# Routed attention with a hard-swish feed-forward: where the range check reads, and what stands between two users of one PSUM bank

## Chip, cores, metric

One core of a Trainium2 chip. The metric is the device time of one execution in microseconds (us), median of several runs. The engines are TensorE (PE, with its weight loads as PEld), VectorE (DVE), ScalarE (ACT), GpSimd (POOL) and SyncE (SP), which issues the transfers.

## The reference

Attention in which a query sees only the keys that share its nearest centroid, then a feed-forward block with a hard-swish:

```python
batch, n_heads, seq, head_dim = (4, 8, 768, 64); n_clusters = 16
n_tokens, d_model, d_ff = (3072, 512, 2048)

q_assign = np.argmax(np.einsum('bhsd,hcd->bhsc', q_n, c_n), axis=-1)
k_assign = np.argmax(np.einsum('bhsd,hcd->bhsc', k_n, c_n), axis=-1)
mask = q_assign[:, :, :, None] == k_assign[:, :, None, :]
scores = scale * np.matmul(q, k.transpose(0, 1, 3, 2))
scores = np.where(mask, scores, -1000000000.0)
attn = np.exp(scores - np.max(scores, axis=-1, keepdims=True))
attn = attn / (np.sum(attn, axis=-1, keepdims=True) + 1e-09)
x = np.matmul(attn, v)                     # (b, h, s, d) -> (b*s, h*d)
h = x @ w_in
g = h * np.clip(h + 3.0, 0.0, 6.0) / 6.0
out = g @ w_out
```

Inputs are float32, the two weight matrices float64.

## The kernel before

`fast_path` does the work without the row maximum, and at the end writes a flag, `ok`. Only where a check of ranges fails does `general_path` run afterwards and do it again in a safe way; it does not run with these inputs.

The heads go in 16 pairs. A pair g has 12 chunks of keys (two halves of the queries, `hf`, by six key tiles, `j`), numbered n = 12 g + 6 hf + j, 192 in all. The main loop takes two chunks in a pass, called a step below; r is n mod 12. The order within each engine is the order in which the program is written (`tc.manual_schedule()`), each engine works through its own list in that order, and the tile framework adds the waits. A step does, in this order:

- `scores` (L349) of the chunks n and n+1: products of queries and keys into `ps`, plus the routing part from `xm`; ScalarE's exponential into `ex` (L356); GpSimd adds `ex` up into `acc` (L360, L363).
- `attn_v` (L367) of the two chunks before: `ex` times the values into `pv`, copied to `num` after six chunks (L379).
- the range check left over from the step before (the list `later`).
- at r = 2 and r = 8, `divide` (L385) for the half that ended: PE sums `acc` over the keys into `pd` (L394), VectorE takes the reciprocal `rcp` (L398) and multiplies `num` with it into `xT` (L399). ScalarE's `in_range` (L406) adds up a copy, called `same`, of `pd` at once, and of `rcp` in the next step. The sums must stay finite and under a bound, which is tested at the end.
- the routing of the next pair ("prep", `prep_items`, L467), in pieces: `turn` (two pieces in each of r = 0 and r = 2, of three transposes each, `pqk`, copied to `xf` by VectorE or ScalarE), `route` (r = 4: 24 narrow matmuls `pr`, then VectorE's argmax into `one_hot`), `route_turn` (two pieces in r = 8 and one in r = 10: four matmuls each, `po`, cast to `xm` by ScalarE, L328).
- feed-forward items of a batch whose attention is done, from a list called `fill` (`ffn_items`, L416): an "up" item is four matmuls into `ph` (L423), ScalarE's Relu `t` (L430) and VectorE's `gT` (L432); a "down" item is four matmuls into `py` (L445). `items_by` (L495) says how many a step gets: none before n = 52, mostly one from n = 52 to 78, four from n = 80 to 98, two or three after that. Prep pieces and items alternate, and the piece comes first (L549 to L553).
- from the start until n = 80 also the weights: loads of float64 chunks and their decoding, two ScalarE passes and five VectorE operations for a chunk (L201 to L230).

PSUM has eight banks. `pd`, `pqk`, `pr` and `po` are short-lived and come from `scratch` (L164): from n = 52 on they share one bank (`psum_t`), one after another; before that every third of them takes this bank and the others take the two banks of the feed-forward items (`psum_m`). A new user of a bank waits until the last reader of the one before is through.

Of the kernel before, what the change touches and what calls it, by code (L numbers as in the profile page):

```python
# [8 lines left out]
F32 = mybir.dt.float32  # L9
BF16 = mybir.dt.bfloat16  # L10
U32 = mybir.dt.uint32
I32 = mybir.dt.int32
ALU = mybir.AluOpType
ACT = mybir.ActivationFunctionType
AX = mybir.AxisListType
# [3 lines left out]
P = 128  # L19
NCH = S // P  # L20
NC2 = 2 * NCH
HALF = S // 2
NHC = NCH // 2
NG = B * H
# [6 lines left out]
NW = NKT * DFF // WC + NFT  # L31
# [3 lines left out]
W_HIGH = 2.0**15  # L35
# [8 lines left out]
BOUND = 2.0**60  # L44
# [72 lines left out]
def fast_path(ctx, tc, ok, q, k, v, centroids, moe_w_in, moe_w_out, out):  # L117


    nc = tc.nc  # L120
    PSUM = bass.MemoryType.PSUM

    def pool(name, bufs, **kw):
        return ctx.enter_context(tc.tile_pool(name=name, bufs=bufs, **kw))

    const = pool("const", 1)
# [4 lines left out]
    smallp = pool("smallp", 2)  # L131
    expp = pool("expp", 4)
    accp = pool("accp", 2)
    nump = pool("nump", 2)
# [16 lines left out]
    ones = const.tile([P, D], F32, name="ones")  # L151
    rank = const.tile([P, C], F32, name="rank")
    half_c = const.tile([P, 1], F32, name="half_c")
    cnT = const.tile([P, H * C], F32, name="cnT")
    one_hot = const.tile([P, NC2, P], BF16, name="one_hot")


    totals = const.tile([P, 2, NG], F32, name="totals")
    w_totals = const.tile([P, 2, NW], F32, name="w_totals")
# [4 lines left out]
    def scratch(shape, name):  # L164

        st["scratch"] += 1
        if st["early"] and st["scratch"] % 3:
            return psum_m.tile(shape, F32, name=name, tag="m")
        return psum_t.tile(shape, F32, name=name, tag="t")
# [3 lines left out]
    def load(g, *names):  # L173
        if g >= NPAIR:
            return
        b, h = divmod(2 * g, H)
        for name in names:
            if name == "v":
                dst = st["v", g] = vp.tile([P, NCH, 2, D], F32, name="vt")
            elif name == "q":  # L180
                st["qk", g] = qkp.tile([P, 2, NCH, 2, D], F32, name="qk")
            if name != "v":
                dst = st["qk", g][:, "qk".index(name)]
            src = {"q": q, "k": k, "v": v}[name]
            for t in range(2):
                nc.sync.dma_start(dst[:, :, t], src[b, h + t].rearrange("(p j) d -> p j d", p=P))
# [9 lines left out]
    def load_weights(i):  # L196
        if i < len(chunks):
            st["raw", i] = rawp.tile([P, WC, 2], U32, name="raw")
            nc.sync.dma_start(st["raw", i], chunks[i][1])
# [37 lines left out]
    def constants():  # L237
        make_identity(nc, ident)
        nc.vector.tensor_copy(out=ident_q, in_=ident)
        nc.vector.tensor_scalar_mul(out=ident_k, in0=ident, scalar1=-FAR)  # L240
        for t in range(2):
            nc.vector.tensor_reduce(
                out=parity[:, t : t + 1],
                in_=ident.rearrange("p (h t c) -> p t h c", t=2, c=C)[:, t], axis=AX.XY, op=ALU.max,
            )
        for c in range(C):
            nc.gpsimd.memset(rank[:, c : c + 1], float(C - c))
        nc.gpsimd.memset(half_c, 0.5)
        nc.gpsimd.memset(ones, 1.0)
        nc.gpsimd.memset(w_low, W_LOW)  # L250
        nc.gpsimd.memset(one_hot, 0.0)

    def centroid_norm():
        cn = unit_rows(nc, smallp, cen, D)

        nc.scalar.activation(out=w_totals[:, 0, 0:1], in_=w_low, func=ACT.Exp)

        wide = smallp.tile([P, 2, D], F32, name="cenwide")
        for t in range(2):
            nc.vector.tensor_scalar_mul(out=wide[:, t], in0=cn, scalar1=parity[:, t : t + 1])  # L260
        pc = scratch([P, P], "pc")
        nc.tensor.transpose(out=pc, in_=wide, identity=ident)
        nc.vector.tensor_copy(out=cnT, in_=pc)
# [67 lines left out]
    def where(n):  # L331
        g, r = divmod(n, 2 * NCH)
        return (g, *divmod(r, NCH))

    def scores_qk(n):
        g, hf, j = where(n)
        st["ps", n] = psum_s.tile([P, 2, 512], F32, name="ps")
        scores_part(n, st["xf", g], True)
# [46 lines left out]
    def divide(n):  # L385
        g, hf, _ = where(n)
        b, kt = divmod(g, NKT)
        if kt == 0 and hf == 0:
            st["xT", b] = xtp.tile([P, NKT, S], F32, name="xT")
        acc, num = st.pop(("acc", g, hf)), st.pop(("num", g, hf))  # L390
        pd = scratch([P, 512], "pd")
        pd = pd[:, 0:HALF]
        for t in range(2):
            nc.tensor.matmul(  # L394
                pd[t * D : (t + 1) * D], lhsT=ones, rhs=acc[:, t], start=True, stop=True
            )
        rcp = nump.tile([P, HALF], F32, name="rcp")
        nc.vector.reciprocal(out=rcp, in_=pd)  # L398
        nc.vector.tensor_tensor(  # L399
            out=st["xT", b][:, kt, hf * HALF : (hf + 1) * HALF], in0=num, in1=rcp, op=ALU.mult  # L400
        )
        in_range(g, hf, 0, pd)
        return lambda: in_range(g, hf, 1, rcp)


    def in_range(g, hf, a, x):  # L406
        same = nump.tile([P, HALF], BF16, name="same", tag="same")
        nc.scalar.activation(  # L408
            out=same, in_=x, func=ACT.Copy, accum_out=totals[:, a, 2 * g + hf : 2 * g + hf + 1]
        )  # L410


# [54 lines left out]
    def prep_items(g, r):  # L467

        if g >= NPAIR:
            return []  # L470
        if r in (0, 2):
            return [lambda: turn(g, r), lambda: turn(g, r + 1)]
        return {
            4: [lambda: route(g)],
            8: [lambda: route_turn(g, 0), lambda: route_turn(g, 1)],
            10: [lambda: route_turn(g, 2)],
        }.get(r, [])
# [27 lines left out]
    fill, later = [], []  # L505
    done = 0

    with tc.manual_schedule():
        nc.scalar.dma_start(cen, centroids.rearrange("h c d -> (h c) d"))
        load(0, "q", "k")  # L510
        constants()
        load(0, "v")
        load_weights(0)
        centroid_norm()
        for part in range(4):
            turn(0, part)
        load(1, "q", "k")
        scores_qk(0)
        scores_qk(1)
        route(0)  # L520
        for part in range(3):
            route_turn(0, part)

        for n in range(0, total + lag_d + 2, 2):
            g, r = divmod(n, per_pair)
            for i in (n, n + 1):
                if i < total:
                    scores(i)
            for i in (n - lag_v, n - lag_v + 1):
                if 0 <= i < total:  # L530
                    attn_v(i)
            for check in later:
                check()
            later = []
            m = n - lag_d + 1
            if m >= 0 and m % NCH == NCH - 1:
                later.append(divide(m))
            if n == READY:
                st["early"] = False
            if m >= 0 and m % per_batch == per_batch - 1:  # L540
                fill += ffn_items(m // per_batch)
            if r == 6:
                load(g + 2, "q", "k")
                load(g + 1, "v")
            prep = prep_items(g + 1, r)
            want = items_by(n + 2) - done if n < total else len(fill)
            want = min(want, len(fill))
            done += want
            for i in range(max(len(prep), want)):  # L549
                if i < len(prep):  # L550
                    prep[i]()
                if i < want:
                    fill.pop(0)()  # L553
            for i in range(chunks_by(n), chunks_by(n + 2)):
                load_weights(i + 1)
                decode_weights(i)
            if n >= total:
                for check in later:
                    check()
                later = []  # L560

    good = smallp.tile([P, 2 * NG], F32, name="good")
    fit = smallp.tile([P, 2 * NW], F32, name="fit")
    nc.vector.tensor_scalar(
        out=good, in0=totals.rearrange("p a n -> p (a n)"), scalar1=BOUND, scalar2=None, op0=ALU.is_le
    )
    for a, bound in enumerate((W_HIGH, 0.0)):
        nc.vector.tensor_scalar(  # L570
            out=fit[:, a * NW : (a + 1) * NW], in0=w_totals[:, a], scalar1=bound, scalar2=None,
            op0=ALU.is_le,
        )
    low = smallp.tile([P, 2], F32, name="low")
    nc.vector.tensor_reduce(out=low[:, 0:1], in_=good, axis=AX.X, op=ALU.min)
    nc.vector.tensor_reduce(out=low[:, 1:2], in_=fit, axis=AX.X, op=ALU.min)
    one = smallp.tile([P, 1], F32, name="one")
    nc.vector.tensor_reduce(out=one, in_=low, axis=AX.X, op=ALU.min)
    pl = psum_t.tile([1, P], F32, name="pl", tag="t")
# [365 lines left out]
```

## Time and profile before

| | |
|---|---|
| median of 3 runs | 1275.11 us (1271.45 to 1277.72) |
| the profiled execution, its own time | 1268.65 us |
| its span, first to last instruction | 1266.7 us |
| mean granted TensorE clock | 0.946 |
| PE busy | 1143.7 us |
| DVE, ACT, POOL busy | 392.8, 362.4, 299.0 us |

The profile is one execution. Its views: busy time by engine; waits, each put down to the instruction that ended it; groups of instructions by source line; the timeline of single instructions; and busy time with the granted TensorE clock for any stretch of time. A clock of 1.00 is 2.4 GHz, 0.50 is 1.2 GHz. Times in the timeline count from the first instruction. A matmul in float32 shows as two records, and the time of one record is longer than its distance to the next, since they are pipelined: the length of a group is read from the start of what follows it.

### The profile page before, as it was taken

Reading aid. Unit: us, or ns where it says so; the run is one execution under the profiler, and the core shown is the slowest. Engines: PE = TensorE matmul, PEld = TensorE weight load, DVE = VectorE, ACT = ScalarE, POOL = GpSimd, SP = SyncE. Lnnn points to the kernel's source line nnn. Section 1 sums busy time; section 2 is a strip of 40 time slices with the busy share of each in tenths; the row PEclk is TensorE's granted clock in tenths of the full one; section 3 lists DMA queues with packets and bytes.
Section 4 is the critical chain, followed back from the end, with each engine's and each line's share of the span. In section 5 each row is a group of like instructions: output and inputs, shape, how many; then the busy total and the mean of one; then the engine's idle time right before and its main releaser. Section 6 shows DMA issues by size and latency. Waiting matters only on the chain.

```text
span 1266.7 us, 11458 instructions
## 1 busy us (share of the span) xinstructions
PE 1143.7 (90%) x4610; PEld 575.1 (45%) x4610; DVE 392.8 (31%) x530; ACT 362.4 (29%) x692; POOL 299.0 (24%) x186
## 2 busy tenths in 40 slices
PE   6988878788989899888998889988899899999997
PEld 4444443334445435454444544545435444554553
DVE  3667886867012211222022211222111221210110
ACT  3555545444112211332223222232222331120110
POOL 3555632323111211221222212122121222000000
PEclk9998978889999999998999989999999999999999
DMA  5322242423001001010010100101000000000000
GB/s 129 82 72 61 71 121 67 121 67 71 8 25 30 1 17 46 1 38 1 17 46 1 38 1 18 46 1 38 1 17 21 1 1 8 17 1 17 9 9 20
DMA packets 83535, 42.81 MB, mean 34 GB/s; under 512 B 76304, under 2 KB 76304, under 8 KB 83472
## 3 DMA queue, kind: packets, MB, share of 16 engines
q1 hardware_dynamic: 83328, 41.95, 12.7%
q8 instruction: 38, 0.62, 0.2%
q14 instruction: 25, 0.20, 0.1%
q10 hardware_dynamic: 144, 0.03, 0.0%
HBM read 35.68 MB, written 6.29 MB: 33 GB/s over the span
## 4 chain that ended last, share of the span: by engine, by line
PE 81%; DVE 16%; ACT 2%; issue 1%; POOL 0%; DVEq 0%; POOLq 0%; ACTq 0%
PE py L445 27%; PE ph L423 27%; PE ps L344 11%; PE pv L373 9%; DVE rcp L398 6%; PE pr L290 3%; PE pqk L276 2%; DVE wunit L227 2%; DVE wunit L223 1%; PE pd L394 1%; DVE wtop L220 1%; DVE w_in_sb L230 1%; ACT same L408 1%; DVE wtop L216 1%; PE po L324 1%; DVE w_out_sb L230 1%
## 5 line engine op out<-in xcount | busy, mean ns | idle before, releaser
L363 POOL TENSOR_TENSOR acc<-acc,ex 128x768 f32<-128x768 f32 x128 | 237.7, 1857 | 557.4 <-ACT ex L356 552.3
L423 PE MATMUL ph<-xT,w_in_sb 128*128 128x384 f32 x1024 | 368.8, 518 | 0.0
L445 PE MATMUL py<-w_out_sb,gT 128*128 128x512 f32 x768 | 349.6, 611 | 0.0
L423 PEld LDWEIGHTS ph<-xT,w_in_sb 128*128 128x128 f32 x1024 | 202.7, 203 | 139.4 <-issue 28.5
L445 PEld LDWEIGHTS py<-w_out_sb,gT 128*128 128x128 f32 x768 | 148.6, 198 | 176.2 <-issue 175.7
L356 ACT ACTIVATE ex<-ps 128x768 f32<-128x768 f32 x192 | 151.5, 808 | 221.6 <-PE ps L344 221.1
L344 PE MATMUL ps<-xf 64*128 64x384 f32 x768 | 173.3, 531 | 7.2 <-ACT ex L356 7.2
L430 ACT ACTIVATE t<-ph,half_c 128x384 f32<-128x384 f32 x128 | 74.3, 580 | 354.5 <-PE ph L423 354.5
L432 DVE SCALAR_TENSOR_TENSOR gT<-t,ph 128x384 f32<-128x384 f32 x128 | 70.8, 554 | 305.7 <-ACT t L430 305.7
L373 PE MATMUL pv<-ex,vt 128*64 128x384 f32 x768 | 147.2, 505 | 0.0
L398 DVE RECIPROCAL rcp<-pd 128x384 f32<-128x384 f32 x32 | 81.8, 2555 | 119.3 <-PE pd L394 119.2
L360 POOL TENSOR_TENSOR acc<-ex 128x768 f32<-128x768 f32 x32 | 58.7, 1834 | 211.5 <-ACT ex L356 211.4
L451 DVE COPY y<-py 128x512 f32<-128x512 f32 x24 | 16.6, 692 | 273.9 <-PE py L445 273.9
L344 PEld LDWEIGHTS ps<-xf 64*128 64x128 f32 x768 | 66.1, 194 | 76.4 <-issue 52.6
L373 PEld LDWEIGHTS pv<-ex,vt 128*64 128x64 f32 x768 | 47.3, 138 | 83.8 <-issue 81.3
L276 PE MATMUL pqk<-ident,qk 128*128 128x128 f32 x192 | 35.7, 314 | 38.5 <-ACT same L408 32.7
L344 PE MATMUL ps<-xm 64*128 64x384 bf16 x384 | 65.6, 336 | 0.3 <-ACT xm L328 0.3
L408 ACT ACTIVATE same<-pd 128x384 bf16<-128x384 f32 x32 | 15.7, 490 | 152.6 <-DVE rcp L398 152.6
L324 PE MATMUL po<-ident_q,one_hot 128*128 128x128 bf16 x96 | 11.2, 243 | 53.1 <-ACT same L408 50.1
L276 PEld LDWEIGHTS pqk<-ident,qk 128*128 128x128 f32 x192 | 24.8, 157 | 66.7 <-ACT same L408 39.4
L290 PEld LDWEIGHTS pr<-cnT,xf 128*128 128x128 f32 x384 | 45.8, 198 | 12.2 <-ACT same L408 5.7
L324 PEld LDWEIGHTS <-one_hot 128*128 128x128 bf16 x192 | 13.9, 104 | 81.9 <-issue 77.9
(67 smaller groups left out, 496.1 us busy)
## 6 DMA issues: line engine op xcount, KB each, us to landing
raw<-in_moe_w_in_dram SPq DMA_DIRECT2D x16, 512.0 KB, 3.7
raw<-in_moe_w_out_dram SPq DMA_DIRECT2D x16, 512.0 KB, 3.5
qk<-in_q_dram SPq DMA_DIRECT2D x32, 192.0 KB, 3.5
qk<-in_k_dram SPq DMA_DIRECT2D x32, 192.0 KB, 4.2
vt<-in_v_dram SPq DMA_DIRECT2D x32, 192.0 KB, 4.4
out_dram<-y SPq DMA_DIRECT2D x24, 256.0 KB, 2.0
cen<-in_centroids_dram ACTq DMA_DIRECT2D x1, 32.0 KB, 1.7
```

The costliest lines, as they stand in the source:

```text
L276: nc.tensor.transpose(out=pt[:, i], in_=qk[:, j // NCH, j % NCH], identity=ident)
L290: nc.tensor.matmul(pr[:, j], lhsT=xf[:, j], rhs=cnT[:, c0 : c0 + 2 * C], start=True, stop=True)
L344: nc.tensor.matmul(st["ps", n][:, t, 0:HALF], lhsT=x[r, NCH + j], rhs=x[r, hf * NHC : (hf + 1) * NHC], start=first, stop=not first,)
L356: nc.scalar.activation(out=ex, in_=sc, func=ACT.Exp, scale=SM_SCALE)
L360: nc.gpsimd.tensor_tensor(out=acc, in0=st["ex", n - 1], in1=ex, op=ALU.add)
L363: nc.gpsimd.tensor_tensor(out=acc, in0=acc, in1=ex, op=ALU.add)
L373: nc.tensor.matmul(pv[t * D : (t + 1) * D], lhsT=vt[:, j, t], rhs=ex[:, t], start=(j == 0), stop=(j == NCH - 1),)
L398: nc.vector.reciprocal(out=rcp, in_=pd)
L423: nc.tensor.matmul(hh, lhsT=w_in_sb[:, kt, f * P : (f + 1) * P], rhs=xT[:, kt, hf * HALF : (hf + 1) * HALF], start=(kt == 0), stop=(kt == ...
L430: nc.scalar.activation(out=t, in_=hh, func=ACT.Relu, bias=half_c, scale=1.0 / 6.0)
L432: nc.vector.scalar_tensor_tensor(out=gT, in0=t, scalar=1.0, in1=hh, op0=ALU.min, op1=ALU.mult)
L445: nc.tensor.matmul(py, lhsT=st["g", f][:, i * P : (i + 1) * P], rhs=w_out_sb[:, f], start=(f == 0), stop=(f == NFT - 1),)
```

## The change

Three things. First, both passes of the range check read `rcp` in SBUF, and both are done in the step after the divide, behind that step's exponentials: a sum of `rcp`, which must stay under the bound, and a sum of Relu(1/BOUND - rcp), which must be 0. `pd` in PSUM is read by the reciprocal alone. Second, in a step the feed-forward item comes first and the prep piece second. Third, the two tests at the end are written as one loop, with a VectorE comparison more. The attention, routing and feed-forward arithmetic is the same.

```diff
@@ constants()
+        nc.gpsimd.memset(low_c, 1.0 / BOUND)
@@ divide(n)
-        in_range(g, hf, 0, pd)
-        return lambda: in_range(g, hf, 1, rcp)
-    def in_range(g, hf, a, x):
+        return lambda: in_range(2 * g + hf, rcp)
+    def in_range(i, rcp):
         same = nump.tile([P, HALF], BF16, name="same", tag="same")
+        nc.scalar.activation(out=same, in_=rcp, func=ACT.Copy, accum_out=totals[:, 0, i : i + 1])
+        lack = nump.tile([P, HALF], BF16, name="lack", tag="same")
         nc.scalar.activation(
-            out=same, in_=x, func=ACT.Copy, accum_out=totals[:, a, 2 * g + hf : 2 * g + hf + 1]
+            out=lack, in_=rcp, func=ACT.Relu, bias=low_c, scale=-1.0, accum_out=totals[:, 1, i : i + 1]
         )
@@ the main loop
             for i in range(max(len(prep), want)):
+                if i < want:
+                    fill.pop(0)()
                 if i < len(prep):
                     prep[i]()
-                if i < want:
-                    fill.pop(0)()
@@ the end
-    good = smallp.tile([P, 2 * NG], F32, name="good")
-    fit = smallp.tile([P, 2 * NW], F32, name="fit")
-    nc.vector.tensor_scalar(
-        out=good, in0=totals.rearrange("p a n -> p (a n)"), scalar1=BOUND, scalar2=None, op0=ALU.is_le
-    )
-    for a, bound in enumerate((W_HIGH, 0.0)):
-        nc.vector.tensor_scalar(
-            out=fit[:, a * NW : (a + 1) * NW], in0=w_totals[:, a], scalar1=bound, scalar2=None,
-            op0=ALU.is_le,
-        )
+    good = smallp.tile([P, 2, NG], F32, name="good")
+    fit = smallp.tile([P, 2, NW], F32, name="fit")
+    for got, sums, high in ((good, totals, BOUND), (fit, w_totals, W_HIGH)):
+        for a, bound in enumerate((high, 0.0)):
+            nc.vector.tensor_scalar(
+                out=got[:, a], in0=sums[:, a], scalar1=bound, scalar2=None, op0=ALU.is_le
+            )
...
```

How this moves instructions, at two places. (The added lines shift the line numbers: L394 is L396 in the changed kernel, L276 is L278, L423 is L426.)

PE at the divide in the step n = 110, one of the steps with three items. Before:

```order
L373 MATMUL pv<-ex,vt 64x384 x4
L394 MATMUL pd<-acc,ones 64x384 x2
L276 MATMUL pqk<-ident,qk 128x128 x3
L423 MATMUL ph<-xT,w_in_sb 128x384 x4
L276 MATMUL pqk<-ident,qk 128x128 x3
L423 MATMUL ph<-xT,w_in_sb 128x384 x8
```

and in the changed kernel:

```order
L375 MATMUL pv<-ex,vt 64x384 x4
L396 MATMUL pd<-acc,ones 64x384 x2
L426 MATMUL ph<-xT,w_in_sb 128x384 x4
L278 MATMUL pqk<-ident,qk 128x128 x3
L426 MATMUL ph<-xT,w_in_sb 128x384 x4
L278 MATMUL pqk<-ident,qk 128x128 x3
L426 MATMUL ph<-xT,w_in_sb 128x384 x4
```

An up item now stands between `pd` and the transposes that take its bank, and one stays between the two groups of transposes.

PE at the divide in the step n = 62, which has one item. Before:

```order
L394 MATMUL pd<-acc,ones 64x384 x2
L276 MATMUL pqk<-ident,qk 128x128 x3
L423 MATMUL ph<-xT,w_in_sb 128x384 x4
L276 MATMUL pqk<-ident,qk 128x128 x3
L344 MATMUL ps<-xf 128x384 x2
```

and in the changed kernel:

```order
L396 MATMUL pd<-acc,ones 64x384 x2
L426 MATMUL ph<-xT,w_in_sb 128x384 x4
L278 MATMUL pqk<-ident,qk 128x128 x6
L346 MATMUL ps<-xf 128x384 x2
```

The one item has gone ahead of both groups, so that nothing is left between them.

## Rows read from the trace of the kernel before

**Rows 1.** The page's head and busy time of PE (share of the span, instructions)

```profile
span 1266.7 us, 11458 instructions
...
PE 1143.7 (90%) x4610; PEld 575.1 (45%) x4610; DVE 392.8 (31%) x530; ACT 362.4 (29%) x692; POOL 299.0 (24%) x186
```

**Rows 2.** PE's waits: line, releaser, us in total, times, longest us

```profile
PE po L324 <- ACT same L408: 55.8, 13, 9.5
PE pqk L276 <- ACT same L408: 32.7, 10, 3.3
PE ps L344 <- ACT ex L356: 7.2, 4, 2.3
...
PE pqk L276 <- DVE xf L281: 5.7, 2, 2.9
...
PE ps L344 <- ACT xm L328: 0.3, 1, 0.3
```

**Rows 3.** Waits of all engines: ScalarE's check

```profile
ACT same L408 <- DVE rcp L398: 152.6, 32, 20.3
```

**Rows 4.** Timeline of one divide (start, us, engine, instruction, idle before and releaser)

```profile
590.85 0.81 PE L394 MATMUL pd<-acc,ones 128*64 128x384 f32 x4
...
591.71 2.56 DVE L398 RECIPROCAL rcp<-pd 128x384 f32<-128x384 f32 x1 [13.06 <-PE pd L394]
594.30 0.49 ACT L408 ACTIVATE same<-pd 128x384 bf16<-128x384 f32 x1 [3.82 <-DVE rcp L398]
...
594.94 0.59 PE L324 MATMUL po<-ident_q,one_hot 128*128 128x128 bf16 x4 [3.27 <-ACT same L408]
```

**Rows 5.** Timeline of PE: an up item, `pr`, two down items

```profile
541.57 2.75 PE L423 MATMUL ph<-xT,w_in_sb 128*128 128x384 f32 x8
544.15 0.49 PE L276 MATMUL pqk<-ident,qk 128*128 128x128 f32 x3
...
567.64 2.87 PE L290 MATMUL pr<-cnT,xf 128*128 128x32 f32 x24
...
580.63 7.13 PE L445 MATMUL py<-w_out_sb,gT 128*128 128x512 f32 x16
587.70 0.92 PE L344 MATMUL ps<-xf 64*128 64x384 f32 x4
```

**Rows 6.** By stretch: us, busy PE, PEld, DVE, ACT, POOL, then clock, DMA

```profile
168.00:307.00 139.00, 107.84 (x504) 55.35 (x500) 105.30 (x145) 68.17 (x152) 41.85 (x22) 0.88 0.36 96
375.00:1004.00 629.00, 579.93 (x2305) 291.68 (x2305) 125.07 (x175) 158.47 (x279) 137.46 (x76) 0.95 0.08 19
1004.00:1092.00 88.00, 88.00 (x306) 40.31 (x306) 12.71 (x16) 18.72 (x33) 19.92 (x12) 1.00 0.02 7
...
594.94:598.36 3.42, 3.42 (x8) 1.84 (x8) 0.00 (x0) 0.58 (x1) 0.00 (x0) 0.51 0.02 5
...
422.52:425.94 3.42, 3.42 (x17) 2.18 (x17) 0.00 (x0) 0.89 (x2) 0.00 (x0) 1.00 0.02 5
...
570.64:574.14 3.50, 3.50 (x7) 1.88 (x6) 2.76 (x6) 0.00 (x0) 0.00 (x0) 0.55 0.00 0
...
541.00:546.00 5.00, 5.00 (x21) 3.14 (x20) 1.11 (x2) 1.43 (x3) 1.61 (x1) 1.00 0.00 0
```

**Rows 7.** Timeline around n = 56, and PE's wait at n = 80

```profile
185.39 0.58 PE L324 MATMUL po<-ident_q,one_hot 128*128 128x128 bf16 x4 [9.41 <-ACT same L408]
...
186.01 0.58 ACT L328 CAST xm<-po 128x512 bf16<-128x512 f32 x1 [0.67 <-PE po L324]
...
312.51 0.59 PE L324 MATMUL po<-ident_q,one_hot 128*128 128x128 bf16 x4 [5.08 <-ACT same L408]
```

**Rows 8.** Timeline before n = 52: ScalarE at a divide, PE at another

```profile
43.26 0.49 ACT L408 ACTIVATE same<-pd 128x384 bf16<-128x384 f32 x1 [3.81 <-DVE rcp L398]
...
77.43 0.39 PE L324 MATMUL po<-ident_k,one_hot 128*128 128x128 bf16 x4 [2.87 <-ACT same L408]
```

**Rows 9.** Groups by line and shape: the check's pass over `rcp` (busy us, mean ns)

```profile
L408 ACT ACTIVATE same<-rcp 128x384 bf16<-128x384 f32 x32 | 16.6, 519 | 0.0
L408 ACT ACTIVATION_READ_ACCUMULATOR same<-rcp 128x1 f32 x32 | 6.3, 198 | 0.0
```

**Rows 10.** Timeline of the end: the first test of the sums, and `pl`

```profile
1217.77 0.20 DVE L566 TENSOR_SCALAR good<-totals 128x64 f32<-128x64 f32 x1
...
1257.65 0.27 PE L580 MATMUL pl<-ident,one 128*1 128x128 f32 x1
```

More of the change, by code (lines that the diff above doesn't have):

```diff
@@ L153, in fast_path @@
     half_c = const.tile([P, 1], F32, name="half_c")
+    low_c = const.tile([P, 1], F32, name="low_c")
     cnT = const.tile([P, H * C], F32, name="cnT")
@@ L560, in fast_path @@
                 later = []
-    good = smallp.tile([P, 2 * NG], F32, name="good")
-    fit = smallp.tile([P, 2 * NW], F32, name="fit")
-    nc.vector.tensor_scalar(
-        out=good, in0=totals.rearrange("p a n -> p (a n)"), scalar1=BOUND, scalar2=None, op0=ALU.is_le
-    )
-    for a, bound in enumerate((W_HIGH, 0.0)):
-        nc.vector.tensor_scalar(
-            out=fit[:, a * NW : (a + 1) * NW], in0=w_totals[:, a], scalar1=bound, scalar2=None,
-            op0=ALU.is_le,
-        )
+    good = smallp.tile([P, 2, NG], F32, name="good")
[5 more added lines that the diff above has]
+            )
     low = smallp.tile([P, 2], F32, name="low")
-    nc.vector.tensor_reduce(out=low[:, 0:1], in_=good, axis=AX.X, op=ALU.min)
-    nc.vector.tensor_reduce(out=low[:, 1:2], in_=fit, axis=AX.X, op=ALU.min)
+    nc.vector.tensor_reduce(out=low[:, 0:1], in_=good, axis=AX.XY, op=ALU.min)
+    nc.vector.tensor_reduce(out=low[:, 1:2], in_=fit, axis=AX.XY, op=ALU.min)
     one = smallp.tile([P, 1], F32, name="one")
```

## Prediction

> **What bounds the kernel now.** I read the page's first part, then TensorE's waits, one divide in the timeline, and the clock by stretches, in that order. TensorE (PE) is busy 90% of the span and the others under a third [rows 1], so time can be won where PE stands still or runs at its lower clock. PE's waits [rows 2] show who holds it: ScalarE's pass `same` (L408) ended 55.8 us of waits before `po` and 32.7 us before `pqk`, in 23 places, out of some 123 us in which PE is idle at all. `same` itself stood 152.6 us behind the reciprocal, in all 32 divides [rows 3]. One divide shows why [rows 4]: PE ends `pd` at 591.66, the reciprocal reads the bank from 591.71 to 594.27, ScalarE reads it after that, not beside it, and at 594.94 the bank is free for `po`: 3.27 us with PE idle. A timeline of PE alone lists the 23: 16 of exactly 3.27 and one of 5.08 from 307 us on, two of 3.27 and two of about 9.4 between 168 and 307 us, two of 2.9 to 2.8 earlier; a wait of 2.6 before `pr` is like them.
>
> The idle time costs twice. In the 3.42 us after that wait PE is granted 0.51 of its clock, close to its lower level of 1.2 GHz [rows 6]; the same view of the stretch after each of the 16 waits of 3.27 gives 0.50 to 0.63 for 15 of them, and 1.00 after 422.52. From 375 to 1004 us the mean is 0.95: 629 x 0.05 = 31 us lost, of which three stretches after `pr` such as 570.64 to 574.14 at 0.55 take 3 x 3.5 x 0.45 = 4.7. About 27 hang on the waits.
>
> **The change, part by part.** A step is one pass of the loop over n, r is n mod 12.
>
> *Stage C, from n=80 (307 to 1004 us).* All 17 divides with a routing piece behind them have three or four feed-forward items in their step. Now an item stands between `pd` and the piece, and another between the two pieces. An up item takes PE from 541.57 to 544.15, 2.58 us; two down items take 7.07, one 3.5 [rows 5]. The bank is free when the reciprocal ends, 2.6 us after `pd`, plus some 0.06: without ScalarE's pass 0.67 earlier than now [rows 4]. So an up item leaves 0.1 us of wait and a down item none. Saved: 16 x 3.27 + 5.08 = 57.4, less about 1 for the up items and 0.9 at n=80, whose reciprocal comes late (5.08 - 0.67 - 3.5 [rows 7]): 55.5 us. The items themselves are not added, only moved, and between two scratch users one item stays. Clock: 27 plus some 3 for n=80 and 86 (before 375 us), of which I take 28, since PE has no gap left there; from 1004 to 1092 us, with PE busy 88.00 of 88, it is 1.00 [rows 6]. C gives 83 us. What is late next is VectorE: the first item's `gT` queues behind reciprocal and `xT`, done some 3.9 us after `pd` (2.6 + 0.6 + 0.6 and gaps); the third item, which needs that item's bank, starts after 5.6 us, so this covers.
>
> *Stage B, n=52 to 78 (168 to 307 us).* Nearly every step has one item only, and two pieces in r = 0, 2, 8. Now the item is ahead of both and the second piece waits for the copy of the first: `po` to the end of its copy is 0.67 + 0.58 after PE's own 0.3 [rows 7], about 0.95 us of new wait. At n=56 and 68 PE waited 9.4, because VectorE was still decoding weights: the item (2.6) and `same` (0.67) come out, 0.95 comes in, -2.3 each. At n=62 and 74: 3.27 becomes 0.1 + 0.95, -2.2 each. At n=60 and 72 the wait for VectorE's copy `xf` was 2.9 each already [rows 2]; the item's `gT` (0.55) now queues ahead of that copy, +0.55 each. Sum -7.9. Clock: 0.88 over 139 us is 16.7 lost [rows 6]; at n=62 and 74 PE's gap falls under 1 us, which I take to return 1.7 each; the 6 us left at n=56 and 68 keep theirs low. B gives 11 us, bounds 0 (VectorE, 76% busy there, sets the pace and PE's gain turns into waits for it) and 17.
>
> *Stage A, before n=52 (40 to 168 us).* No items exist, so the order stays; only the check moves. ScalarE no longer stands behind the reciprocal ahead of its casts and exponentials (3.81 us at 43.26 [rows 8]). The four waits of scores for `ex`, 7.2 us in all [rows 2], came from that; I take all of them, and 0.67 from each of three waits for `same` (77.43 is one [rows 8]), and 2 for the clock. A gives 11 us; bounds 2 (only the 0.67s) and 14.
>
> *The new check.* Still two ScalarE passes in each of 32 divides, now both two steps' work later, behind that step's exponentials. The Relu pass is not in the trace with this shape; the nearest row, the Copy from the same tile, is 519 ns and its read-out 0.2 [rows 9], so about 0.7 us stands in front of that step's `t` or casts. With an item's 2.6 us on PE ahead of them this is hidden; in A, without items, it could cost up to 0.7 x 8 = 5.6, inside A's bounds. One more small VectorE comparison at the end sits at 1217.77, 40 us before the last chain `pl` at 1257.65 [rows 10]: nothing. A memset of one column more at the start: nothing, behind other memsets.
>
> Sum: 83 + 11 + 11 = 105 us. The profiled execution took 1268.65 us, 6.5 under the median 1275.11; the waits recur in every execution, so I take them off the median: **1170 us**.
>
> **The rivals.** *R1, the gap closes but the clock does not come back.* In 8 of C's 17 divides the piece behind the gap is six small transposes, in r = 2, and small pieces stay close together. After `pr`, of 24 narrow matmuls, the clock falls in three pairs though PE had no gap [rows 5, 6]. If the r = 2 divides stay low: 8 x 1.5 = 12 us, 1182; if all 17: 28 us, 1198. Against it: from 541 to 546 us, r = 0, both `pqk` pieces run between items at a clock of 1.00 [rows 6], the very order that r = 2 now gets. The Trainium skill's "TensorE: Matmul & The Clock Gate", Part 4 on PE-mode transposes, says that a transpose does not count as PE being busy in the same way, so that full clock does not engage for it: by that rule R1 is the outcome, with the 1182; the 1.00 of that row speaks against it as long as items surround the transposes.
>
> *R2, the single bank hands the wait on.* In steps with one item the two pieces now meet, and if VectorE's queue (decode, `gT`) stands in front of the copy as it did for 2.9 us at n=60, six steps of B pay up to 3 us instead of 0.95: 6 x 2 = 12, and B turns from -11 to about 0. With A at its lower end too the time is 1170 + 11 + 9 = 1190.
>
> *R3, the change does not do what it says:* the moved item cannot start in the gap, because its own bank or weights are late. Then only the 0.67 of 24 waits and A's exponentials go, 16 + 7: 1252. Against it: the item's two banks are a different pool, and no wait of PE for `t` or `gT` stands among its waits.
>
> *R4, slower: the prep becomes the chain.* Every routing piece now starts one item later. If what it feeds were needed at once, PE would stand for that item: 5 prep steps x 8 pairs in C x 3 us = 120, against 105 saved: 1290. It decides where the slack behind a piece is under one item, 2.6 us. The trace has `pr` at 567.64 and its first user `po` at 594.94 [rows 4, 5], 27 us later, and scores waited for `xm` 0.3 us once in all [rows 2].
>
> **How the numbers follow.** Forecast 0.78; R1 0.12; R2 0.05; R3 0.03; R4 0.02. Forecast's own bounds: C idle 52 to 57, C clock 22 to 33 (the three `pr` stretches may go or be joined by others), A 2 to 14, B 0 to 17; not all at one end, so 1153 to 1187. The range reaches on to R1's far end and R2, 1152 to 1198, and leaves out R3, R4 and the corner where all terms are low. A measurement here tells about 0.5% (6 us) from no change. Faster by more than that: the first four cases, 0.98, less 0.02 for R3 with A's part gone too: 0.96; same 0.02; slower, R4, 0.02.
>
> **What would show it.** Right: waits of PE for ScalarE's check gone from the list; in C nothing longer than 0.3 us between `pd` and the piece; clock near 0.99 from 307 us to the end of C, which should last about 614 us instead of 697; in B waits of `po` and `pqk` for `xm` and `xf` of about 1 us, six of them, and 6 us at n=56 and 68; in A no waits for `ex`. Wrong: low clock after r = 2 divides (R1), long waits for `xf` (R2), `pd` followed by idle time with the item behind it (R3), waits of scores for `xm` or of `po` for `one_hot` (R4).

## The result and the profile after

Predicted 1170 us, in 1152 to 1198; measured 1165.38 us median (1162.96 to 1167.33) against 1274.67 for the kernel before: a ratio of 0.914, 95% interval 0.911 to 0.917. The profiled execution took 1166.84 us, its span is 1164.7, its mean clock 0.977 (0.946 before).

The waits of PE in the changed kernel, in the columns of [rows 2]:

```profile
PE po L326 <- DVE rcp L400: 15.1, 2, 9.1
PE pqk L278 <- DVE xf L283: 8.8, 4, 3.1
...
PE ps L346 <- ACT ex L358: 4.8, 2, 3.2
PE po L326 <- DVE one_hot L314: 4.6, 3, 3.0
PE pqk L278 <- DVE rcp L400: 3.3, 1, 3.3
PE po L326 <- ACT xm L330: 1.3, 2, 0.7
PE pr L292 <- DVE rcp L400: 0.9, 1, 0.9
PE ps L346 <- ACT xm L330: 0.3, 1, 0.3
```

ScalarE's check, 55.8 and 32.7 us in [rows 2], is gone. What is left lies before n=80. The largest, 15.1 us in two places, is the reciprocal that VectorE reaches late at n=56 and 68.

The stages are cut at the start of four reciprocals, those of n=8, 50, 80 and 182, which both kernels have. Busy time and clock by stretch, in the columns of [rows 6], A, B, C and the rest, for the kernel before:

```profile
40.67:153.98 113.31, 100.44 (x634) 49.69 (x634) 80.58 (x84) 64.18 (x132) 68.31 (x37) 0.94 0.29 74
153.98:309.30 155.32, 119.69 (x552) 63.14 (x549) 121.17 (x163) 75.85 (x170) 47.94 (x25) 0.87 0.34 93
309.30:1021.51 712.21, 656.65 (x2565) 326.78 (x2565) 136.70 (x189) 174.10 (x305) 152.77 (x85) 0.95 0.07 18
1021.51:1266.70 245.19, 236.41 (x681) 116.93 (x681) 36.94 (x57) 31.86 (x59) 14.46 (x8) 0.99 0.03 10
```

and for the changed one:

```profile
40.72:149.29 108.57, 98.84 (x640) 49.45 (x639) 94.51 (x84) 67.33 (x137) 70.16 (x37) 0.97 0.29 75
149.29:292.08 142.79, 116.66 (x547) 59.50 (x546) 111.74 (x163) 74.94 (x165) 46.23 (x24) 0.88 0.39 103
292.08:918.85 626.77, 626.77 (x2565) 310.21 (x2566) 135.78 (x188) 173.58 (x305) 153.98 (x85) 1.00 0.08 21
918.85:1164.70 245.85, 236.41 (x681) 116.69 (x681) 37.11 (x58) 32.16 (x59) 14.47 (x8) 0.99 0.03 10
```

C lost 85.4 us: PE's idle time there, 712.2 - 656.7 = 55.6, is now 0.00, and the same 2565 records take 29.9 us less, since the clock went from 0.95 to 1.00. B lost 12.5, of which 9.5 idle time, A 4.7, and the rest is 0.7 longer: 102 us in all.

These cuts are made by VectorE, which is late at some reciprocals, so they move a few us between neighbouring stages: 1.87 of the 5.08 us that PE waited at n=80 fall into B here, and so does the wait of 2.6 before `pr`, which the prediction counts in A. Cut at the start of PE's `pd` of the same n instead (39.81, 149.70, 306.62 and 1020.65 us before, 39.85, 143.35, 291.22 and 917.99 after), A lost 6.4 us, B 9.0 and C 87.3.

One divide of C, n=110, in the changed kernel's timeline, to be held against [rows 4]:

```profile
509.67 0.81 PE L396 MATMUL pd<-acc,ones 128*64 128x384 f32 x4
510.42 2.85 PE L426 MATMUL ph<-xT,w_in_sb 128*128 128x384 f32 x8
510.53 2.56 DVE L400 RECIPROCAL rcp<-pd 128x384 f32<-128x384 f32 x1 [3.07 <-PE pd L396]
...
513.15 0.55 PE L278 MATMUL pqk<-ident,qk 128*128 128x128 f32 x3
```

The up item fills PE from 510.42, the reciprocal ends at 513.09, the transposes begin at 513.15. That is 2.73 us after the item began, against 2.58 where no bank is waited for [rows 5]: a wait of some 0.15 us that the profile does not list, since the records of matmuls overlap. A divide of B with one item, n=62:

```profile
204.48 2.56 DVE L400 RECIPROCAL rcp<-pd 128x384 f32<-128x384 f32 x1 [3.22 <-PE pd L396]
...
207.09 0.55 PE L278 MATMUL pqk<-ident,qk 128*128 128x128 f32 x3
...
207.86 0.55 DVE L435 SCALAR_TENSOR_TENSOR gT<-t,ph 128x384 f32<-128x384 f32 x1 [0.23 <-ACT t L433]
208.33 0.55 DVE L283 COPY xf<-pqk 128x384 f32<-128x384 f32 x1
...
208.94 0.55 PE L278 MATMUL pqk<-ident,qk 128*128 128x128 f32 x3 [1.30 <-DVE xf L283]
```

Here the second piece meets the first, and waits 1.30 us for its copy, which stands behind `gT`.

### The profile page after: what moved, and what is told of

The parts are those of the page before. It is cut to its first block, busy times and chain, and to the rows that moved or that the text cites. A ratio compares the mean times of both kernels' runs of the same rounds, so it can differ in the third digit from the quotient of the medians.

```text
span 1164.7 us, 11468 instructions
## 1 busy us (share of the span) xinstructions
PE 1109.2 (95%) x4610; PEld 554.4 (48%) x4610; DVE 396.6 (34%) x531; ACT 364.4 (31%) x692; POOL 300.3 (26%) x187
## 4 chain that ended last, share of the span: by engine, by line
PE 86%; DVE 12%; ACT 1%; issue 0%; DMA 0%; POOL 0%; DVEq 0%; POOLq 0%; ACTq 0%; SPq 0%
PE py L448 29%; PE ph L426 28%; PE ps L346 13%; PE pv L375 9%; PE pr L292 3%; DVE wtop L221 2%; DVE rcp L400 2%; PE pqk L278 2%; DVE wunit L228 2%; PE pd L396 1%; DVE wunit L224 1%; DVE wtop L217 1%; PE po L326 1%; DVE w_in_sb L231 1%; DVE one_hot L314 1%
## 5 line engine op out<-in xcount | busy, mean ns | idle before, releaser
L426 PE MATMUL ph<-xT,w_in_sb 128*128 128x384 f32 x1024 | 350.1, 492 | 0.0
L448 PE MATMUL py<-w_out_sb,gT 128*128 128x512 f32 x768 | 341.9, 597 | 0.0
L426 PEld LDWEIGHTS ph<-xT,w_in_sb 128*128 128x128 f32 x1024 | 188.0, 190 | 142.9 <-issue 27.2
L448 PEld LDWEIGHTS py<-w_out_sb,gT 128*128 128x128 f32 x768 | 141.7, 190 | 172.8 <-issue 172.3
L346 PE MATMUL ps<-xf 64*128 64x384 f32 x768 | 176.8, 540 | 4.8 <-ACT ex L358 4.8
L330 ACT CAST xm<-po 128x512 bf16<-128x512 f32 x48 | 27.4, 583 | 74.5 <-PE po L326 74.5
L292 PE MATMUL pr<-cnT,xf 128*128 128x32 f32 x384 | 44.8, 274 | 0.9 <-DVE rcp L400 0.9
L281 ACT COPY xf<-pqk 128x384 f32<-128x384 f32 x32 | 15.3, 479 | 95.0 <-PE pqk L278 95.0
L278 PE MATMUL pqk<-ident,qk 128*128 128x128 f32 x192 | 32.3, 292 | 12.1 <-DVE xf L283 8.8
L278 PEld LDWEIGHTS pqk<-ident,qk 128*128 128x128 f32 x192 | 24.2, 149 | 35.4 <-issue 16.5
```

What stands on the lines that cost most here:

```text
L278: nc.tensor.transpose(out=pt[:, i], in_=qk[:, j // NCH, j % NCH], identity=ident)
L292: nc.tensor.matmul(pr[:, j], lhsT=xf[:, j], rhs=cnT[:, c0 : c0 + 2 * C], start=True, stop=True)
L346: nc.tensor.matmul(st["ps", n][:, t, 0:HALF], lhsT=x[r, NCH + j], rhs=x[r, hf * NHC : (hf + 1) * NHC], start=first, stop=not first,)
L426: nc.tensor.matmul(hh, lhsT=w_in_sb[:, kt, f * P : (f + 1) * P], rhs=xT[:, kt, hf * HALF : (hf + 1) * HALF], start=(kt == 0), stop=(kt == ...
L448: nc.tensor.matmul(py, lhsT=st["g", f][:, i * P : (i + 1) * P], rhs=w_out_sb[:, f], start=(f == 0), stop=(f == NFT - 1),)
```

## The experiments

The theory: C's gain is the item in the gap, idle time and clock together; the check's move adds 0.67 us of each gap and unblocks ScalarE. The main rival: the bank was held by ScalarE's pass, and the item only fills. Ratios are to the kernel before, run beside each group.

**Only the order** (the kernel before, with the item first):

```diff
+                if i < want:
+                    fill.pop(0)()
                 if i < len(prep):
                     prep[i]()
-                if i < want:
-                    fill.pop(0)()
```

> The kernel before with the feed-forward item put first, the range check as it was (a pass over pd at once, a pass over rcp in the next step). Theory: the item in the gap does nearly all of the work. In C (n=80 and on) the bank is free 0.67 us later than in the changed kernel, behind ScalarE's pass: 3.27 us after pd, which a down item (3.5 us) covers and an up item (2.58) misses by 0.7; 9 of C's 17 divides have an up item, so 6 us of idle time against none, and no low clock. Stage A (before n=52) as in the kernel before, 4.7 us longer than in the changed one, B about 2.7 longer. Sum 1165 + 6 + 5 + 3 = 1179 us, ratio to before 0.925. Rival (the check's move is what frees the bank, the item only fills): the waits for ScalarE's pass stay over 2 us and the time is over 1230.

Measured: ratio 0.934 (0.928 to 0.940), 1185.5 us. C takes 632.3 us, 5.5 longer than in the changed kernel, against 6 expected. Its waits, the first and the last of nine, all at divides with an up item:

```profile
361.35 0.55 PE L276 MATMUL pqk<-ident,qk 128*128 128x128 f32 x3 [0.50 <-ACT same L408]
...
909.37 0.38 PE L324 MATMUL po<-ident_q,one_hot 128*128 128x128 bf16 x4 [0.49 <-ACT same L408]
```

B takes 147.4 us (4.6 longer) and A 114.9. The order alone makes about three quarters of the gain (0.066 of 0.086 in the ratios), and the rival falls.

**Only the check** (the changed kernel, with the piece first):

```diff
+                if i < len(prep):
+                    prep[i]()
                 if i < want:
                     fill.pop(0)()
-                if i < len(prep):
-                    prep[i]()
```

> The changed kernel with the prep piece first again, as before: only the range check is moved. Theory: the gap in C becomes 3.27 - 0.67 = 2.6 us, now waiting for the reciprocal: 17 x 0.67 = 11 us saved in C, 3 in B, 4.7 in A: 1256 us, ratio 0.985, with the clock low behind nearly every gap as before. Rival 1 (a gap of 2.6 us no longer costs the clock): another 25 us go, 1231. Rival 2 (the bank was never held by ScalarE's pass): 1270 and more.

Measured: ratio 0.975 (0.968 to 0.981), 1236.2 us: between the theory's 0.985 and its first rival (1231 us, a ratio of 0.966), and neither lies in the interval. C takes 689.6 us: idle time fell by 10.4, as expected from 16 gaps of 2.66 instead of 3.27 and one of 4.32 instead of 5.08 at n=80, but PE's busy time fell too, from 656.7 to 644.5, since only 11 of the 17 gaps were now followed by a low clock (16 of 17 before). The stretches after three of the gaps of 2.66 us:

```profile
404.26:407.68 3.42, 3.42 (x17) 2.17 (x17) 0.54 (x1) 0.95 (x2) 0.00 (x0) 1.00 0.02 5
457.04:460.46 3.42, 3.42 (x7) 1.87 (x8) 1.12 (x2) 0.00 (x0) 0.00 (x0) 0.53 0.00 0
...
914.62:918.04 3.42, 3.42 (x7) 1.87 (x8) 1.12 (x2) 0.00 (x0) 0.00 (x0) 0.50 0.00 0
```

So the shorter gap gave part of the clock back, which I had as an either-or. How much varies from run to run: the four runs took 1230.5, 1231.8, 1240.6 and 1241.1 us, at mean clocks of 0.964 in the first two and 0.959 and 0.958 in the others, and the trace is that of the second. A took 103.5 us, 9.8 less than before, where 4.7 was expected. But before n=52 there are no items, so this kernel's order in A is the changed kernel's own, and the order-only kernel's is that of the kernel before. The same order thus took from 103.5 to 108.6 us in four traces, and 113.3 and 114.9 in two. Three of them, in the columns of [rows 6]: the order-only kernel, the check-only kernel, and a second profile of the changed kernel (taken with the runs further down):

```profile
42.11:157.03 114.92, 99.01 (x610) 48.74 (x608) 80.59 (x86) 64.39 (x132) 66.19 (x35) 0.91 0.29 75
...
43.19:146.68 103.49, 94.86 (x612) 46.78 (x608) 91.82 (x85) 64.38 (x131) 67.76 (x35) 0.97 0.30 81
...
42.01:147.14 105.13, 97.57 (x616) 48.23 (x613) 90.40 (x85) 64.55 (x131) 67.71 (x35) 0.95 0.30 80
```

A's length can be read to about 5 us and no better.

**The item first only at divides** (with r = 0, 4 and 10 as before):

```diff
-                if i < want:
+                if later and i < want:
                     fill.pop(0)()
                 if i < len(prep):
                     prep[i]()
+                if not later and i < want:
+                    fill.pop(0)()
```

> The changed kernel with the item first only in steps that have a divide (r = 2 and 8); in r = 0, 4 and 10 the piece comes first as before. Theory: all of C's gain comes at the divides, so C keeps it; the three low-clock stretches behind pr (r = 4) return, 3 x 1.6 = 5 us, if the item between the scores and pr is what kept the clock up; B's two steps at r = 0 win back 0.55 us each. 1169 us. Rival (the low clock behind pr was chance, or the idle time elsewhere): no low stretch behind pr, 1164 us. If the item between the two pieces in r = 0 mattered more than thought, over 1175.

Measured: ratio 0.924 (0.919 to 0.929), 1172.7 us. B takes 144.6 us, 1.8 longer where 1.1 shorter was expected. C takes 630.7 us, 3.9 longer than in the changed kernel, with no wait of PE and 0.99 of the clock. The stretch after one of the three `pr` at which the clock is low again, and after one at which it is not:

```profile
365.13:368.63 3.50, 3.50 (x12) 2.07 (x11) 3.08 (x7) 0.58 (x1) 0.00 (x0) 1.00 0.00 0
...
527.02:530.52 3.50, 3.50 (x7) 1.78 (x7) 2.75 (x6) 0.00 (x0) 0.00 (x0) 0.53 0.00 0
```

Over the five traces so far, `pr` straight behind the scores is followed by a low clock in C in 3 of 8 cases (before), 3 of 8 (here) and 1 of 8 (only the check); behind an item in 0 of 8 in each of the two others, and in none of 40 in the five traces below in which the weights are decoded by n=80. The item ahead of `pr` is thus worth some 4 us, which the forecast had not counted (its bounds for the clock allow for it).

**Without GpSimd's additions** before n=48 (the sums of the first batch lack the chunks j = 2 to 5):

```diff
-        elif j > 1:
+        elif j > 1 and g > 3:
             acc = st["acc", g, hf]
```

> The changed kernel without GpSimd's additions of the chunks j = 2 to 5 in the first four pairs (the sums of the first batch leave out these chunks): 32 additions of 1.86 us less, all before n=48. Question: why stage A won 4.7 us and not 11. Theory: VectorE's decoding runs slower beside GpSimd's additions (wtop L221 1522 ns in A where the same operation takes 690 without them), its busy time in A rose from 80.6 to 94.5 us, and so the reciprocals came late. Without the additions VectorE's decode operations fall to about 0.4 to 0.7 us, its busy time in A to about 60, the waits for rcp in A (3.3, and ScalarE's 11.7) vanish and A takes about 99 us instead of 108.6: total 1156. Rival (the reciprocals are late for the order of VectorE's list or for the weights' transfers): VectorE may be faster but A stays within 2 us of 108.6, total 1164.

Measured: ratio 0.907 (0.902 to 0.912), 1152.0 us. A takes 94.9 us, 13.7 less. VectorE's groups of one decode operation in A, with the additions:

```profile
L221 DVE SCALAR_TENSOR_TENSOR wtop<-raw,wtop 128x512 uint32<-128x512 uint32 x9 | 13.7, 1522 | 0.3
L224 DVE TENSOR_SCALAR wunit<-wtop 128x512 uint32<-128x512 uint32 x9 | 12.8, 1422 | 0.3
```

and without:

```profile
L221 DVE SCALAR_TENSOR_TENSOR wtop<-raw,wtop 128x512 uint32<-128x512 uint32 x9 | 6.2, 693 | 0.3
...
L224 DVE TENSOR_SCALAR wunit<-wtop 128x512 uint32<-128x512 uint32 x9 | 3.8, 427 | 0.3
```

PE has no idle time left in A (94.86 busy of 94.86) and ScalarE no wait for `rcp`. From `pd` to `pd` A is 9.8 us shorter. So the additions are what kept A long, and the groups show how: VectorE's decoding is slower beside them. Two waits of ScalarE's exponential for the additions (5.3 us in the changed kernel) went with them; PE had not waited behind either. This kernel leaves work out and is not one to use.

**The check a step later still:**

```diff
-            for check in later:
+            for check in due:
                 check()
-            later = []
+            due, later = later, []
...
```

> The changed kernel with the two passes of the range check one step later still. Theory: in stage A ScalarE still stands 11.7 us in all before the check, since the reciprocals are late there, and the exponentials behind it make the scores wait (4.8 us); with the check a step later both go, and A wins up to 4 us, nothing elsewhere: 1161 against 1165 us. Rival (A is paced by VectorE, which decodes beside GpSimd's additions): ScalarE's 11.7 us go, A keeps its 108.6 us, total 1165.

Measured: ratio 0.914 (0.911 to 0.916), 1162.2 us, beside 0.915 (0.912 to 0.918) for the changed kernel in the same group. ScalarE's 11.7 us behind `rcp` (8.9 in the changed kernel's own profile of this group) fell to 1.2, and the waits for `ex` in A went. In their place PE stood 1.7 us for `rcp` and 4.7 for `xf`, both VectorE's work. A took 104.8 us, and 105.1 in the changed kernel's profile of this group; the `pd` of n=80 starts at 287.5 us in both. The rival holds.

**Decoding behind the divide** (chunks of r = 0 and 6 a step later):

```diff
...
-            for i in range(chunks_by(n), chunks_by(n + 2)):
+            held += range(chunks_by(n), chunks_by(n + 2))
+            while held and (r not in (0, 6) or n >= DECODED - 2):
+                i = held.pop(0)
                 load_weights(i + 1)
                 decode_weights(i)
```

> The changed kernel with the weight chunks of the steps r = 0 and 6 (those just ahead of a divide) decoded in the step after, behind the divide. Theory: what is left of idle time in B at n=56 and 68 (9.1 and 6.1 us before po) is VectorE's decoding ahead of the reciprocal; with the decoding behind it the two waits fall to under 1 us, some other waits for VectorE grow (pr and xf, 3 us), so B falls from 142.8 to about 133; A's wait of 3.3 us for rcp at n=32 goes too. 1154 us. Rival (VectorE is the pace of B, whatever its order): the waits move to xf and one_hot and B stays within 2 us: 1165.

Measured: ratio 0.916 (0.913 to 0.919), 1166.2 us. PE's waits for `rcp` are gone, and others have taken their place:

```profile
PE pqk L278 <- DVE xf L283: 15.1, 4, 6.3
PE ps L346 <- ACT ex L358: 9.1, 4, 3.4
...
PE po L326 <- DVE one_hot L314: 6.2, 5, 3.0
PE py L448 <- DVE gT L435: 3.8, 1, 3.8
```

B takes 145.4 us, no less than the 142.8. My expectation fell. The rival, that VectorE's load paces B whatever its order, fits, but no run takes that load off B, so it is argued and not shown.

**Both (the check later and the decoding behind the divide), and the piece first in steps of one item, two pieces and no divide:**

```diff
...
+            first = later or want >= len(prep)
...
-                if i < want:
+                if first and i < want:
                     fill.pop(0)()
...
+                if not first and i < want:
+                    fill.pop(0)()
...
```

> Both edits of the two kernels before this one, and in steps of one item, two pieces and no divide (n=60 and 72) the piece first, then the item, then the second piece. If they add up: 1165 - 4 - 11 - 1 = 1149 us. If VectorE paces A and B: 1163.

Measured: ratio 0.912 (0.909 to 0.915), 1159.2 us. This is the lowest median of the kernels that leave nothing out, 3.6 us under that of the changed kernel beside it (1162.8). Five of its six runs are faster than all six of the changed kernel and the sixth is not: a gain of 0.3% is likely, but not settled.

> The changed kernel itself, as it is, on the same chip as the three kernels with it: 1165 us, ratio 0.914.

Measured: 0.915 (0.912 to 0.918), 1162.8 us.

**Decoding spread over more steps:**

```diff
-    DECODED, READY = 5 * per_batch // 3, per_batch + lag_d
+    DECODED, READY = 92, per_batch + lag_d
```

> The changed kernel with the weights decoded by n=92 instead of n=80 (the number DECODED alone): about one chunk in a step instead of one or two, 16 up items spread to n=92 and the other 40 of the first batch in four steps of ten. Theory: VectorE's decoding is what B waits for (po behind rcp 15.1 us, pqk behind xf 8.8). With one chunk ahead of a reciprocal the waits of 9.1 and 6.1 us fall to under 2, the low clock behind them goes; against it, 3 more steps have one item between the divide and two pieces or none at all (n=62: 2.7 us of gap). Net 10 us: 1154. Rival (the waits only spread, as with the decoding moved behind the divide): 1163 to 1165.

Measured: ratio 0.920 (0.917 to 0.923), 1170.7 us.

> The same with n=86. Theory: about half of that gain, 1159. Rival: 1163 to 1165.

Measured: ratio 0.921 (0.919 to 0.924), 1173.3 us.

> Decoding until n=92, the check one step later, and the piece first in steps of one item, two pieces and no divide. Theory: 1154 less some 2 us for the check and 1 for the order: 1151. Rival: 1160 and more.

Measured: ratio 0.916 (0.913 to 0.918), 1166.1 us. All three missed: none has a ratio below the changed kernel's. From the reciprocal of n=50 to that of n=104, by which point both have done the same items, the changed kernel takes 330.6 us and these 334.1, 336.0 and 332.7. With n=92 the waits of 9.1 and 6.1 us fell to 1.5 and 3.9 (under 2 expected), and one of 3.9 came up at n=80. PE waits in 15 places from 150 to 301 us, where the changed kernel has 9 from 149 to 292: more steps have one item, so that the two pieces meet, or none, as n=52 and 62, which have their gap back. In sum these waits are no longer (24.1 us against 26.1 between the two reciprocals). What grew is PE's busy time for the same work, from 304.5 to 310.0 us, since the clock is low behind more of them: `pr` of n=52, the first line here, takes 5.33 us, and 2.87 in the changed kernel. The first and the last of the 15 waits, and the gap of n=62:

```profile
150.88 5.33 PE L292 MATMUL pr<-cnT,xf 128*128 128x32 f32 x24 [5.14 <-DVE rcp L400]
...
196.69 0.55 PE L278 MATMUL pqk<-ident,qk 128*128 128x128 f32 x3 [2.66 <-DVE rcp L400]
...
300.66 0.55 PE L278 MATMUL pqk<-ident,qk 128*128 128x128 f32 x3 [1.30 <-DVE xf L283]
```

## Why the prediction was right

*The bound and the mechanism.* Right: the bank between `pd` and its next user was the wait, the item covers it, and the order alone shows that the item, not the check, does most.

*Stage C, 83 forecast, 85.4 measured (87.3 from `pd` to `pd`).* The listed waits of 57.4 us are all gone, where 55.5 were forecast to go. The 0.9 us expected to stay at n=80 did not, as its reciprocal was in time (`pd` ends at 292.03, the reciprocal starts at 292.08); the 0.1 us behind each up item came, hidden in overlapping records. That the first table has 55.6 beside the 55.5 is chance, since its cut lies inside the wait at n=80. The clock gave 29.9 us, and 28 was forecast: right in size, not in its make-up. I expected the three low stretches behind `pr` to stay, and they went too (3.9 us by the run with the item first only at divides), so the gaps themselves gave some 26.

*Stage B, 11 forecast, 12.5 measured (9.0 from `pd` to `pd`).* The six waits that were to shrink by 7.9 us shrank by 5.9. At n=56 nothing was won: 9.41 us became 9.05 for `rcp` and 0.67 for `xm`, so there PE's gain did turn into a longer wait for VectorE, as in my lower bound. At n=68 9.46 became 6.08 and 0.67, as forecast. At n=62 and 74 1.30 for `xf` stayed (0.95 forecast, and 0.1 before it), at n=60 and 72 3.08 (3.4 forecast). With the decoding reordered or spread out, nothing more came.

*Stage A, 11 forecast, 4.7 measured (6.4 from `pd` to `pd`, 8.2 in the second profile).* The length leaves room, since one order's traces differ by 5 us; the waits do not. The forecast took away 9.2 us of them, 7.2 for `ex` and 0.67 three times, and 4.8 went: 2.4 for `ex` and 4.0 at the three waits for the check, less 1.6 of new waits for `one_hot`. The step that failed is "I take all of them", on the four waits for `ex`: 4.8 of 7.2 us stayed, two instead of four. ScalarE was no longer held at the divide but still at the check a step on, where the reciprocal was late (11.7 us in two places); and with that wait taken away as well, the time did not fall. The pace there is VectorE, whose busy time rose from 80.6 to 94.5 us for the same 84 operations, beside GpSimd's additions (80.6 and 90 to 95 in the other traces of the two orders); with the additions out, A fell by 13.7 us. My sum took VectorE's durations as fixed.

*The sum and the range.* C gave some 4 us more than its forecast, and A and B together some 6 less; that the total came out within 5 us of 1170 owes something to this. The range's lower end of 1153 is not what its sentence says: it is the corner with all terms at their best (1275 - 90 - 14 - 17 = 1154).

*The new check.* Right: the Relu pass takes 603 ns, its read-out 190, hidden in C, where PE has no idle time at all.

*The rivals.* R1 did not happen: from 292 to 919 us the clock is 1.00, with 32 groups of transposes in the stretch. The rule of the Trainium skill's "TensorE: Matmul & The Clock Gate", Part 4, that full clock does not engage for a transpose, is not borne out by this trace, where the transposes stand between other matmuls. R2 happened in part, in B (1.30 for `xf` instead of 0.95, and 3.08), without costing B its gain. R3 and R4 did not: PE starts the item right behind `pd`, and scores waited 0.3 us for `xm`, as before.

## What to carry to other kernels

Where one PSUM bank passes between short users, put independent matmul work between any two of them, at least as long as the slowest reader; here an item of 2.6 us against a reciprocal of 2.56 is just enough, and that move alone brought about three quarters of the gain. Count the clock with the gap: in C each 2 us of idle time removed gave about 1 us more, though not in proportion (the check alone took away 10.4 us of idle time and 12.2 of busy time, and the run with decoding until n=92 lost busy time while its idle time fell). Where VectorE decodes beside GpSimd's additions, don't add up durations from the trace as if they were fixed: when an edit lets the two run together, the operations themselves grow.

## What the runs showed of the hardware that was not expected

In these traces a shorter gap costs the clock less often, not less deeply: in C, after gaps of 3.27 us (the kernel before) the granted clock was low in 15 of 16 cases, after 2.66 us (only the check) in 10 of 16, after 0.5 us (only the order) in none of 9. Where it was low, the mean of the stretch was 0.50 to 0.66, so that it was at the 1.2 GHz level for the better part. Each count is of one execution, and the check-only kernel's runs differ by 10 us, so the middle one is not exact.

VectorE's operations that take 0.4 to 0.7 us alone take about 2 when they meet a GpSimd addition. In the changed kernel's timeline in A, four additions in a row, VectorE's decoding beside them, and behind it the late reciprocal for which ScalarE's check waits:

```profile
65.76 7.95 POOL L365 TENSOR_TENSOR acc<-acc,ex 128x768 f32<-128x768 f32 x4 [1.51 <-ACT ex L358]
65.83 2.04 DVE L217 TENSOR_SCALAR wtop<-raw 128x512 uint32<-128x512 uint32 x1
...
67.91 2.19 DVE L221 SCALAR_TENSOR_TENSOR wtop<-raw,wtop 128x512 uint32<-128x512 uint32 x1
...
70.13 1.92 DVE L224 TENSOR_SCALAR wunit<-wtop 128x512 uint32<-128x512 uint32 x1
...
72.08 2.18 DVE L228 SCALAR_TENSOR_TENSOR wunit<-raw,wunit 128x512 f32<-128x512 uint32 x1
...
74.91 2.55 DVE L400 RECIPROCAL rcp<-pd 128x384 f32<-128x384 f32 x1
77.49 0.52 ACT L409 ACTIVATE same<-rcp 128x384 bf16<-128x384 f32 x1 [7.49 <-DVE rcp L400]
```

Four operations, each about as long as one addition (1.99 us). The Trainium skill's "SBUF — State Buffer", section "Who interferes with whom", says that the two engines share a pair of ports, which the instruction that takes it holds for its whole length while the other engine stands; the trace agrees, one VectorE operation to one addition. Only the additions' effect on VectorE was tested, by leaving them out.

What stays open is how to shorten A and B without leaving work out: they still hold 36 us of PE's idle time, and six kernels that reorder the decoding, the check or both moved it without shortening the whole by more than the 0.3% of one of them.
